# Feature tiles that overlap in the middle, and B turned straight from DRAM, in a fused S5 scan and gated unit

## The chip, the cores and the metric

One core of one Trainium2 chip runs the kernel. The metric is device time in microseconds (us) of one execution, as the median of several. The engines are TensorE (PE in the profile, its weight loads PEld), VectorE (DVE), ScalarE (ACT), GpSimd (POOL) and SyncE (SP), which issues nearly all DMAs.

## The reference

2048 tokens of 448 features are normalised; one branch runs a diagonal complex recurrence (S5) over them, the other a gated unit of width 1792; the output joins both.

```python
xn = layernorm(A_x)                                # [1, 2048, 448], bfloat16
# S5: Lam_bar = exp(dt*Lam); B_bar = ((Lam_bar-1)/Lam)[:, None] * (B_re + 1j*B_im)
Bu = einsum("bld,pd->blp", xn, B_bar)
h[t] = Lam_bar * h[t-1] + Bu[t]                    # over 2048 tokens
s = 2 * einsum("blp,dp->bld", h, C_re + 1j*C_im).real + xn * Dskip
# gated unit
z = (sigmoid(xn @ w_gate) * (xn @ w_up)) @ w_down
out = A_x + s * silu(z)
```

## The kernel before

The tokens are cut into four chunks of 512 (`NCH`, `TC`), each of four token tiles of 128. For each chunk the kernel makes: the normalised tokens `xn` (tokens on partitions), the same turned, `xnT` (features on partitions, 448 of them as `KT` = 4 tiles), 14 blocks of the gated unit (`gu_unit`, block `ft` = 128 of the 1792 columns: products `g_ps` and `u_ps`), 4 units of B times x (`bu_unit`, written -1 to -4: products `bu`), the scan and its rotations on DVE (`bu_after`), the product with `w_down` (`emit_downs`, `d_ps`) and the product with C (`emit_ys`, `y_ps`).

**The four feature tiles.** 448 is three tiles of 128 and a rest of 64. Tiles 0 to 2 are features 0 to 383. Tile 3 holds features 384 to 447 twice, on partitions 0 to 63 and again on 64 to 127, so that the gate's rest can be multiplied from the upper half of the array and the up projection's from the lower. For this the last 64 columns of `xn` are copied to columns 448 to 511 before turning: in `ln_turn` (line 272, DVE for token tiles 0 and 1 and POOL for 2 and 3 of chunk 0) and in `ln_twice` (line 277; DVE for chunk 1, ACT for chunks 2 and 3). The weights lie accordingly: `wg` and `wu` hold rows 0 to 383 as three tiles, `wt` holds the gate's last 64 rows on partitions 0 to 63 and up's on 64 to 127.

**Turning.** Chunk 0 is turned by TensorE (line 274) into PSUM and copied out by DVE (`ln_out`, line 282); chunks 1 to 3 by DMA transposes from SBUF (line 270). B is loaded into SBUF (`load_rows`, tiles `b_re`, `b_im` under the tags `raw_re` and `raw_im`), doubled on ACT (`emit_b_twice`) and turned by eight DMA transposes (`emit_b`, line 297) into `bT`. C is loaded raw under the tags `raw_c` (c_re) and `raw_re` (c_im), turned by two sets of four DMA transposes into `tc_re` and `tc_im` (line 169), and then mixed into `ct` by `emit_c`: ACT makes a temporary (`c_tmps`, line 482) and DVE adds (line 483). The first two temporaries of `emit_c` take the room of tag `raw_im`, the third and fourth that of another pool, the fifth and sixth that of `raw_c`.

**Products in halves.** Most products use 64 of the 128 rows of the array, and a product of the upper half runs beside one of the lower. A sum in PSUM (`Sum`, line 504) takes products of both halves. Where it changes halves, a word is passed: an empty instruction in POOL's queue waits for the last product of the one half, and the first product of the other waits for it.

```python
if self.half not in (None, half):
    word = pool.nop()
    tc.add_manual_dep(word.ins, self.ins.ins.name, SYNC, reason="the other half's last product")
    tc.add_manual_dep(m.ins, word.ins.name, SYNC, reason="the other half's last product")
```

**Order.** Every engine runs its instructions in the written order (`keep_order`). `duo` makes two units at a time: the first half of the one beside the second half of the other, then the reverse. Chunk 0 runs blocks 0 to 3 in the prologue and then the pairs of `emit_line`; chunks 1 to 3 run theirs with the down product of the chunk before after the second pair:

```python
emit_line(0, ((4, 5), (6, 7), (-1, 8), (-2, 9), (-3, 10), (11, 12), (-4, 13)))
```
```python
emit_line(c, ((0, -1), (1, -2), emit_downs, (2, 3), (4, -3), (5, 6), (-4, 7), (8, 9), (10, 11), *ends))
```

`at(c, ft, cost, fn)` hangs other work behind a block: second-chunk normalisation behind (0, 7), small constants of the recurrence on POOL behind blocks 6 to 13 of chunk 0, the turns of C behind (1, 0) and (1, 1), the normalisation of chunk 2 and then three `emit_c` in the down product ("down0", "down1"). PSUM has eight banks, handed out in turn; the four `d_ps` of a down product are therefore the banks of the next pair but one, (4, -3). They are emptied by eight ACT copies (lines 764 and 766).

**Loads on SP.** In order: x of chunk 0, first weight part (columns 0 to 511, four transfers, line 122 and 126), B (four transfers), second part (512 to 1023), x of chunk 1, a turn of B, part of the third weights (1024 to 1791), another turn, the rest of the third part, skip, four turns of B, x of chunk 2; then, behind (0, 7), two turns of `xn` for chunk 1, the last two turns of B, two more of `xn`, `wd`, the raw C, the swaps `bsw` of unit -4 (line 530), and the turns of C.

Of the kernel before, what the change touches and what calls it, by code (L numbers as in the profile page):

```python
# [10 lines left out]
FP32 = mybir.dt.float32  # L11
# [6 lines left out]
D = 448  # L18
F = 1792
# [8 lines left out]
CP = D // KT  # L28
NT = S_TOK // P
NPK = 2 * D  # L30
EPS = 1e-5
TWO_PI = 2.0 * math.pi
HALF_PI = 0.5 * math.pi
# [5 lines left out]
def swap_pair(ap: bass.AP) -> bass.AP:  # L39
    step_p, n_p = ap.ap[0]  # L40
    step_m, n_m = ap.ap[1]
    step_f, n_f = ap.ap[2]
    assert n_m == 2
    return bass.AP(tensor=ap.tensor, offset=ap.offset + step_m,
                   ap=[[step_p, n_p], [-step_m, n_m], [step_f, n_f]])


def bcast_mid(ap: bass.AP, n: int) -> bass.AP:
# [15 lines left out]
def kernel(  # L64
# [48 lines left out]
    skip = w.tile([P, D], BF16, name="skip")  # L113


    def load_rows(eng, t, mat, f0, f1):
        eng.dma_start(out=t[:, 0:3, f0:f1], in_=mat[0:384, f0:f1].rearrange("(kt p) f -> p kt f", p=P))
        eng.dma_start(out=t[0:64, 3, f0:f1], in_=mat[384:448, f0:f1])

    def load_w(eng, f0, f1, between=None):  # L120
        for t, mat in ((wg, B_w_gate), (wu, B_w_up)):
            eng.dma_start(out=t[:, :, f0:f1], in_=mat[0:384, f0:f1].rearrange("(kt p) f -> p kt f", p=P))
        if between:
            between()
        for mat, p0 in ((B_w_gate, 0), (B_w_up, 64)):
            eng.dma_start(out=wt[p0:p0 + 64, f0:f1], in_=mat[384:448, f0:f1])

    pool.memset(ident[:], 0.0)
    pool.affine_select(out=ident[:], in_=ident[:], compare_op=ALU.not_equal, fill=1.0, base=0,  # L129
# [17 lines left out]
            x_t.append(w.tile([P, TPC, D], BF16, name="x3", tag="tc_re"))  # L147
        sync.dma_start(out=x_t[c][:], in_=x_src[:, c * TPC:(c + 1) * TPC, :])

    for nm, mat in (("b_re", A_B_re), ("b_im", A_B_im)):  # L150
        raw[nm] = w.tile([P, KT, DP], BF16, name=nm, tag="raw" + nm[1:])
        load_rows(sync, raw[nm], mat, 0, D)
    dve.memset(raw["b_re"][:, :, D:DP], 0.0)
    load_w(sync, 512, 1024)
    load_x(1)

    ctr = {}
# [98 lines left out]

    def ln_norm(c, j):
        t = c * TPC + j
        xb = xn[c % 3]
        if c < 2:  # L260
            dve.tensor_scalar(out=xb[:, j, 0:D], in0=x_t[c][:, j, :], scalar1=mv[:, t, 0:1],
                              scalar2=rsd[:, t, :], op0=ALU.subtract, op1=ALU.mult)
        else:
            act.activation(xb[:, j, 0:D], x_t[c][:, j, :], ACT.Identity, bias=nmr[:, t, :],
                           scale=rsd[:, t, :])

    def ln_turn(c, j):
        xb, cols = xn[c % 3], slice(j * P, (j + 1) * P)
        if c > 0:
            sync.dma_start_transpose(out=xnT[c][:, 0:KT, cols], in_=xb[:, j, :])  # L270
            return
        (dve if j < 2 else pool).tensor_copy(out=xb[:, j, D:DP], in_=xb[:, j, 384:D])
        for kt in range(KT):
            pe.transpose(tps[j % 2][:, kt, :], xb[:, j, kt * P:(kt + 1) * P], ident[:])  # L274

    def ln_twice(c, copy, j0=0, j1=TPC):
        copy(out=xn[c % 3][:, j0:j1, D:DP], in_=xn[c % 3][:, j0:j1, 384:D])
        for j in range(j0, j1):
            ln_turn(c, j)

    def ln_out(j):
        dve.tensor_copy(out=xnT[0][:, :, j * P:(j + 1) * P], in_=tps[j % 2][:])  # L282

    def emit_b_twice():
        t = raw["b_im"]
        act.copy(out=t[:, 0:3, D:DP], in_=t[:, 0:3, 384:D])
        act.copy(out=t[0:64, 3, D:DP], in_=t[0:64, 3, 384:D])

    def emit_b(cc, pt):
        n = P if pt < 3 else 64
        if cc == 0:
            p0 = pt * P
        else:
            p0 = D if pt == 3 else 512 + pt * P
        sync.dma_start_transpose(out=bT[:, :, p0:p0 + n], in_=raw[("b_re", "b_im")[cc]][0:n, pt, :])

    def bu_cols(pt, cc):
        if pt == 3:  # L300
            return 384, 512
        return (pt * P, (pt + 1) * P) if cc == 0 else (512 + pt * P, 512 + (pt + 1) * P)

# [100 lines left out]

    def emit_skip(c):

        t = xn[c % 3][:, :, 0:D]
        dve.tensor_tensor(out=t, in0=t, in1=bcast_mid(skip[:], TPC), op=ALU.mult)  # L410

# [45 lines left out]
    def emit_c(i):  # L457
        pt = i // 2
        tre, tim = ctr["c_re"][:, pt, :], ctr["c_im"][:, pt, :]
        if pt == 3:  # L460
            ta, sa, tb, sb = tre, K["cr3"][:, 0:1], tim, K["nci2"][:, 3:4]
        elif i % 2 == 0:
            ta, sa, tb, sb = tre, K["cr2"][:, pt:pt + 1], tim, K["nci2"][:, pt:pt + 1]
        else:
            ta, sa, tb, sb = tim, K["ncr2"][:, pt:pt + 1], tre, K["nci2"][:, pt:pt + 1]

        if not c_room:
            for nm in ("raw_im", "raw_c"):
                both = []
                c_room.extend((nm, both, k) for k in range(2))  # L470
                if nm == "raw_im":
# [10 lines left out]
        act.activation(tmp, tb, ACT.Copy, scale=sb)  # L482
        return lambda: dve.scalar_tensor_tensor(out=ct[:, i, :], in0=ta, scalar=sa, in1=tmp, op0=ALU.mult, op1=ALU.add)
# [49 lines left out]
    def bu_unit(c, pt):  # L533
# [2 lines left out]
        sums = [Sum(t, 7) for t in psts]  # L536

        def ops(h, cc, n):
            lo, hi = bu_cols(pt, cc)
            return [(sums[cc], (bT[HALF[h], kt, lo:hi], xnT[c][HALF[h], kt, :], 0, TC))  # L540
                    for kt in range(n)]

        if pt < 3:
            u.top = ops(0, 0, 4) + ops(0, 1, 3)
# [146 lines left out]

    def gu_halves(c, ft, gt, ut, first, n0=0, n1=TC):
        f0, f1 = ft * P, (ft + 1) * P
        for t, p0 in ((gt, 0), (ut, 64)):
            pe.matmul(t[:, n0:n1], lhsT=wt[p0:p0 + 64, f0:f1],  # L695
                      rhs=xnT[c][p0:p0 + 64, 3, n0:n1], start=first, stop=not first)

    def gu_wholes(c, ft, gt, ut, first, n0=0, n1=TC, which=(0, 1)):
        f0, f1 = ft * P, (ft + 1) * P
        for t, wm in [((gt, wg), (ut, wu))[i] for i in which]:  # L700
            for kt in range(3):
                pe.matmul(t[:, n0:n1], lhsT=wm[:, kt, f0:f1], rhs=xnT[c][:, kt, n0:n1],  # L702
                          start=(first and kt == 0), stop=(not first and kt == 2))


    def gu_out(ft, gt, ub):
# [11 lines left out]
    def gu_unit(c, ft):  # L718
# [5 lines left out]

        def ops(h, i, tail):
            x = xnT[c]
            o = [(sums[i], ((wg, wu)[i][HALF[h], kt, f], x[HALF[h], kt, :], 0, TC)) for kt in range(3)]
            return o + [(sums[i], (wt[HALF[h], f], x[HALF[h], 3, :], 0, TC))] * tail

        u.top = ops(0, 0, 1) + ops(0, 1, 0)  # L730
        u.bot = ops(1, 0, 0) + ops(1, 1, 1)
# [57 lines left out]

    def y_ops(c, j, rows, d0=0, d1=D, skipped=False):  # L790
        sl = slice(j * P, (j + 1) * P)
        o = [(ident[rows, :], xn[c % 3][rows, j, d0:d1], d0, d1)] if skipped else []
# [20 lines left out]

    def emit_two(c, j):

        xb, two = xn[c % 3][:, j:TPC:2, 0:D], slice(j, TPC, 2)
        o = op_.tile([P, 2, D], BF16, name="o_t")
        for i in range(2):
            dve.tensor_tensor(out=o[:, i, :], in0=ys[c, j + 2 * i][:], in1=xb[:, i, :], op=ALU.add)  # L819
# [7 lines left out]

    def emit_rest_of(c, j):
        t = op_.tile([P, D], BF16, name="t_g", tag="zb", bufs=4)
        dve.tensor_tensor(out=t[:], in0=xn[c % 3][:, j, 0:D], in1=gs[c][:, j, :], op=ALU.mult)  # L830
        if j % 2 == 0:
            room_of_rests.append(w.tile([P, 2, D], FP32, name="t_x", tag=("raw_re", "raw_im")[j // 2]))
# [62 lines left out]
    def ln_plan(c):  # L895
# [16 lines left out]
        at(own, "down0", 0.0, lambda: ln_twice(c, act.copy))  # L912

    dummy = w.tile([P, 1], FP32, name="dummy")
    act.activation(dummy[:], hpi[:], ACT.Exp)
# [59 lines left out]
    for pt in (0, 1, 3):  # L975
        emit_sin(pt)
        emit_cos(pt)
        if pt == 0:
            emit_neg(pt)
        if pt == 0:  # L980
            emit_b_twice()
    ubs = [fp.tile([P, TC], BF16, name="ub") for _ in range(4)]

    def up_copy(ft):
# [17 lines left out]
    for t in (TPC, TPC + 2):  # L1002
# [1 line left out]
        ln_stats(t + 1)  # L1004
        ln_var(t, 2)
        emit_mul()
    emit_b(0, 0)
    load_w(sync, 1024, F, lambda: emit_b(1, 0))
    sync.dma_start(out=skip[:], in_=A_Dskip.partition_broadcast(P))
    for pt in range(1, KT - 1):  # L1010
        for cc in range(2):
            emit_b(cc, pt)
    load_x(2)


    def second_chunk(j0):
        ln_pow(TPC + j0, 2)
        for j in (j0, j0 + 1):
            ln_norm(1, j)
        ln_twice(1, dve.tensor_copy, j0, j0 + 2)  # L1020

    at(0, 7, 1.0, lambda: second_chunk(0))
    at(0, 7, 0.0, lambda: [emit_b(cc, KT - 1) for cc in range(2)])
    at(0, 7, 1.0, lambda: second_chunk(2))
    at(0, 7, 0.0, lambda: sync.dma_start(out=wd[:], in_=B_w_down.rearrange("(ft p) d -> p ft d", p=P)))
    at(0, 7, 0.0, lambda: load_c("c_re", A_C_re, A_C_im))
# [123 lines left out]
```

## Time and profile before

| what | value |
|---|---|
| time, median of 3 runs | 184.43 us (184.3 to 184.78) |
| span of the profiled execution | 182.6 us |
| median less that span (before the first and behind the last instruction) | 1.83 us |
| busy: PE / DVE / ACT / POOL | 177.7 / 165.0 / 114.1 / 24.5 us |
| prologue, before the first product in halves | 14.2 us |
| granted TensorE clock | 1.000 |
| DMA, SP's queue | 27,632 packets, 14.79 MB |

Times of single instructions count from the start of the span of the profiled execution. The runs' times also hold what lies on both sides of the span; the table's third row is that difference. A line of the timeline gives start, duration, engine, source line, operation, output and inputs, shapes and count, and in brackets the idle time of the engine before it and what ended it. "SPq" is SP issuing a DMA: its duration is the issue, not the transfer. A line of the waits gives who waited for whom, the total, the number of times and the longest.

### The profile page before, as it was taken

The page shows a single profiled execution, that of the slowest core. Times are in us where ns is not written, and L with a number is a line of the kernel's source. Part 1 is how long each engine was busy: PE and PEld are TensorE (multiplying, and loading weights), DVE is VectorE, ACT ScalarE, POOL GpSimd, SP SyncE. Part 2 cuts the span into 40 slices and gives each one's busy share as a digit, 9 for nine tenths or more (in the row PEclk, how much of TensorE's full clock was granted, in tenths as well). Part 3 has the DMA queues.
Part 4 walks back from the last instruction along what each step waited for, and adds up shares of the span by engine and source line. Part 5 has one row for each costly group of instructions (what it writes and reads, how often), then busy time and mean ns, then how long its engine had stood idle before and what let it go on. Part 6 is the DMA issues. An engine that isn't in the chain of part 4 may idle for free.

```text
span 182.6 us, 4348 instructions
## 1 busy us (share of the span) xinstructions
PE 177.7 (97%) x1644; PEld 98.3 (54%) x1644; DVE 165.0 (90%) x337; ACT 114.1 (63%) x236; POOL 24.5 (13%) x61
## 2 busy tenths in 40 slices
PE   7999999999999999999999999999999999999992
PEld 7776644446654444645654445545665544645552
DVE  4899999799989979999999999599999999699983
ACT  3999577979487787997367766057048567144100
POOL 4768546321000000004000000000000000000000
PEclk9999999999999999999999999999999999999999
DMA  5999997895434113011251010030001000011112
GB/s 152 312 307 252 231 161 106 229 311 111 104 76 89 29 32 101 4 52 52 41 79 29 4 29 0 4 101 0 4 2 29 4 13 17 4 50 50 29 36 68
DMA packets 27659, 15.07 MB, mean 83 GB/s; under 512 B 16243, under 2 KB 27638, under 8 KB 27638
## 3 DMA queue, kind: packets, MB, share of 16 engines
q1 hardware_dynamic: 27632, 14.79, 35.1%
q8 instruction: 13, 0.21, 0.5%
q14 instruction: 8, 0.07, 0.2%
q10 hardware_dynamic: 6, 0.00, 0.0%
HBM read 8.49 MB, written 1.84 MB: 57 GB/s over the span
## 4 chain that ended last, share of the span: by engine, by line
PE 97%; DVE 1%; POOL 0%; issue 0%; POOLq 0%; DVEq 0%
PE g_ps L510 25%; PE u_ps L510 19%; PE d_ps L510 17%; PE bu L510 12%; PE y_ps L510 11%; PE d_ps L1093 6%; PE warm_ps L192 2%; PE g_ps L702 2%; PE u_ps L702 1%; PE tp_x L274 1%; PE g_ps L695 1%; DVE sg L846 0%; DVE o_l L852 0%; DVE xnT L282 0%; POOL ident L129 0%
## 5 line engine op out<-in xcount | busy, mean ns | idle before, releaser
L510 PE MATMUL u_ps<-xnT,wu 64*128 64x512 bf16 x312 | 68.9, 376 | 0.0
L510 PE MATMUL g_ps<-xnT,wg 64*128 64x512 bf16 x312 | 62.0, 376 | 0.0
L740 ACT ACTIVATE sig<-g_ps 128x512 bf16<-128x512 f32 x52 | 29.1, 597 | 29.1 <-PE g_ps L510 29.1
L510 PE MATMUL bu<-xnT,bT 64*128 64x512 bf16 x196 | 45.7, 376 | 0.0
L510 PEld LDWEIGHTS <-wu 64*128 64x128 bf16 x312 | 25.3, 94 | 17.8 <-POOLq L512 1.6
L510 PE MATMUL d_ps<-wd,hF 64*128 64x448 bf16 x336 | 32.9, 349 | 0.0
L510 PEld LDWEIGHTS <-wg 64*128 64x128 bf16 x312 | 22.7, 94 | 17.6 <-POOLq L512 1.9
L740 ACT CAST ub<-u_ps 128x512 bf16<-128x512 f32 x52 | 29.3, 604 | 0.8 <-DVE hF L712 0.8
L510 PEld LDWEIGHTS <-hF 64*128 64x128 bf16 x336 | 19.9, 94 | 12.1
L510 PEld LDWEIGHTS <-bT 64*128 64x128 bf16 x196 | 17.7, 94 | 10.7
L510 PE MATMUL y_ps<-ct,h 64*128 64x448 bf16 (+2 forms) x203 | 22.7, 343 | 0.0
L589 DVE TENSOR_TENSOR_SCAN wv<-r_col,st,ta 128x512 bf16<-128x512 f32 x18 | 22.6, 1274 | 0.1
L737 DVE TENSOR_TENSOR hF<-sig,ub 128x512 bf16<-128x512 bf16 x52 | 20.9, 416 | 1.3 <-ACT ub L740 1.1
L510 PE MATMUL u_ps<-xnT,wt 64*128 64x512 bf16 x52 | 19.6, 376 | 0.0
L510 PE MATMUL g_ps<-xnT,wt 64*128 64x512 bf16 x52 | 19.6, 376 | 0.0
L510 PEld LDWEIGHTS <-h 64*128 64x128 bf16 (+1 forms) x203 | 13.4, 95 | 8.0
L570 ACT CAST bus<-bu 128x512 bf16<-128x512 f32 x24 | 14.3, 595 | 2.3 <-PE g_ps L510 2.3
L764 ACT ACTIVATE sigd<-d_ps 128x448 bf16<-128x448 f32 x12 | 6.6, 550 | 12.4 <-PE d_ps L510 12.4
L238 POOL TENSOR_TENSOR rsd<-ve,mhalf 128x1 f32<-128x1 f32 (+2 forms) x8 | 7.5, 932 | 48.5 <-PE u_ps L510 45.6
L510 PEld LDWEIGHTS <-wt 64*128 64x128 bf16 x104 | 9.8, 94 | 5.5 <-DMA wt<-in_B_w_up_dram 0.4
L1093 PE MATMUL d_ps<-wd,hF 128*128 128x448 bf16 x56 | 10.9, 353 | 0.0
L819 DVE TENSOR_TENSOR o_t<-y_ps,xn 128x448 bf16<-128x448 f32 x12 | 6.9, 618 | 3.7 <-PE y_ps L510 3.7
(153 smaller groups left out, 229.8 us busy)
## 6 DMA issues: line engine op xcount, KB each, us to landing
wd<-in_B_w_down_dram SPq DMA_DIRECT2D x1, 1568.0 KB, 7.6
x<-in_A_x_dram SPq DMA_DIRECT2D x3, 448.0 KB, 5.5
out_dram<-o_t SPq DMA_DIRECT2D x6, 224.0 KB, 2.1
wg<-in_B_w_gate_dram SPq DMA_DIRECT2D x2, 384.0 KB, 4.4
wu<-in_B_w_up_dram SPq DMA_DIRECT2D x2, 384.0 KB, 5.3
wg<-in_B_w_gate_dram SPq DMA_DIRECT2D x1, 576.0 KB
wu<-in_B_w_up_dram SPq DMA_DIRECT2D x1, 576.0 KB, 8.6
bsw<-bus SPq DMA_DIRECT2D x8, 64.0 KB, 2.0
```

The source lines that it names most:

```text
L192: pe.matmul(warm_ps[:], lhsT=ident[:], rhs=ident[:], start=True, stop=True)
L238: pool.tensor_tensor(out=rsd[:, t:t + n, :], in0=ve[:, t:t + n, :], in1=mhalf[:, 0:n, :], op=ALU.pow)
L274: pe.transpose(tps[j % 2][:, kt, :], xb[:, j, kt * P:(kt + 1) * P], ident[:])
L510: m = pe.matmul(self.t[:, n0:n1], lhsT=lhsT, rhs=rhs, start=self.done == 1, stop=self.done == self.n)
L570: empty = [lambda cc=cc: act.copy(out=bus[:, cc, :], in_=pst[cc][:]) for cc in range(2)]
L589: dve.tensor_tensor_scan(out=T["wv"][:, cc, :], data0=rb, data1=T["ta"][:, cc, :], initial=(0.0 if c == 0 else st[pt][:, cc, :]), op0=mul, ...
L702: pe.matmul(t[:, n0:n1], lhsT=wm[:, kt, f0:f1], rhs=xnT[c][:, kt, n0:n1], start=(first and kt == 0), stop=(not first and kt == 2))
L737: dve.tensor_tensor(out=h[:], in0=sig[:], in1=ub[:], op=ALU.mult)
L740: u.empty = [lambda: act.activation(sig[:], gt[:], ACT.Sigmoid), lambda: act.copy(out=ub[:], in_=ut[:])]
L764: act.activation(sigd[:], ds[j][:], ACT.Sigmoid)
L819: dve.tensor_tensor(out=o[:, i, :], in0=ys[c, j + 2 * i][:], in1=xb[:, i, :], op=ALU.add)
L1093: pe.matmul(ds[j][:], lhsT=hF[c, ft][:, j * P:(j + 1) * P], rhs=wd[:, ft, :], start=ft == 0, stop=ft == FT - 1)
```

## The change

The four feature tiles start at features 0, 128, 192 and 320 (`K_ROWS`), each 128 long, so that tiles 1 and 2 share features 192 to 255. The gate uses tiles 0, 2 and 3 whole and the upper half of tile 1 (features 128 to 191); up uses tiles 0, 1 and 3 whole and the lower half of tile 2 (features 256 to 319). Nothing is doubled by a copy any more: chunk 0's transposes read overlapping columns of `xn`; for chunks 1 to 3 the normalisation writes 512 columns (features 0 to 255, then 192 to 447) in one instruction with two overlapping runs. Skip, gate and sum read `xn` as two runs of 224. The weights' rows are rearranged to match, and one part is six transfers instead of four.

B is not loaded to SBUF: four DMA transposes read DRAM, each all 448 rows and 256 columns (tiles 0 and 1, or 2 and 3, of one of B_re and B_im). Two POOL copies behind block 9 of chunk 0 gather the last 64 columns of both into `b3` for unit -4. The second weight part is columns 512 to 1279 and stands ahead of x of chunk 1; the third, 1280 to 1791, stands behind the four turns of B. With B's raw tiles gone, `emit_c`'s first two temporaries take tag `raw_re`, and one of the last chunk's temporaries takes `raw_c`.

```diff
+HD = D // 2
+K_ROWS = (0, 128, 192, 320)
+GATE_K, UP_K = (0, 2, 3), (0, 1, 3)
+def two_runs(ap: bass.AP, step: int, n: int) -> bass.AP:
+    return bass.AP(tensor=ap.tensor, offset=ap.offset, ap=[*ap.ap[:-1], [step, 2], [1, n]])
...
+    def load_w(eng, f0, f1):
...
+        eng.dma_start(out=wg[:, 1:3, f0:f1], in_=rows(B_w_gate, 192, 448))
+        eng.dma_start(out=wg[:, 0, f0:f1], in_=rows(B_w_gate, 0, 128))
+        eng.dma_start(out=wu[:, 0:2, f0:f1], in_=rows(B_w_up, 0, 256))
+        eng.dma_start(out=wu[:, 2, f0:f1], in_=rows(B_w_up, 320, 448))
+        eng.dma_start(out=wt[0:64, f0:f1], in_=rows(B_w_gate, 128, 192))
+        eng.dma_start(out=wt[64:128, f0:f1], in_=rows(B_w_up, 256, 320))
...
-    for nm, mat in (("b_re", A_B_re), ("b_im", A_B_im)):
-        raw[nm] = w.tile([P, KT, DP], BF16, name=nm, tag="raw" + nm[1:])
-        load_rows(sync, raw[nm], mat, 0, D)
-    dve.memset(raw["b_re"][:, :, D:DP], 0.0)
-    load_w(sync, 512, 1024)
+    load_w(sync, 512, 1280)
...
+            xb, src = two_runs(xb, 2 * P, 2 * P), two_runs(src, 192, 2 * P)
...
-        (dve if j < 2 else pool).tensor_copy(out=xb[:, j, D:DP], in_=xb[:, j, 384:D])
         for kt in range(KT):
-            pe.transpose(tps[j % 2][:, kt, :], xb[:, j, kt * P:(kt + 1) * P], ident[:])
+            pe.transpose(tps[j % 2][:, kt, :], xb[:, j, K_ROWS[kt]:K_ROWS[kt] + P], ident[:])
-    def ln_twice(c, copy, j0=0, j1=TPC):
-        copy(out=xn[c % 3][:, j0:j1, D:DP], in_=xn[c % 3][:, j0:j1, 384:D])
...
+    def emit_b(cc, kt):
+        sync.dma_start_transpose(out=bT[:, kt:kt + 2, cc * D:(cc + 1) * D],
+                                 in_=(A_B_re, A_B_im)[cc][:, K_ROWS[kt]:K_ROWS[kt] + 2 * P])
+    b3 = w.tile([P, KT, P], BF16, name="b3")
+    def emit_b3():
+        for cc in range(2):
+            pool.tensor_copy(out=b3[:, :, cc * 64:(cc + 1) * 64], in_=bT[:, :, cc * D + 384:(cc + 1) * D])
...
-            for nm in ("raw_im", "raw_c"):
+            for nm in ("raw_re", "raw_c"):
...
-        if pt == 0:
-            emit_b_twice()
...
-    emit_b(0, 0)
-    load_w(sync, 1024, F, lambda: emit_b(1, 0))
+    for cc in range(2):
+        for kt in (0, 2):
+            emit_b(cc, kt)
+    load_w(sync, 1280, F)
     sync.dma_start(out=skip[:], in_=A_Dskip.partition_broadcast(P))
-    for pt in range(1, KT - 1):
-        for cc in range(2):
-            emit_b(cc, pt)
     load_x(2)
...
     at(0, 7, 1.0, lambda: second_chunk(0))
-    at(0, 7, 0.0, lambda: [emit_b(cc, KT - 1) for cc in range(2)])
+    at(0, 9, 0.0, emit_b3)
     at(0, 7, 1.0, lambda: second_chunk(2))
```

More of the change, by code (lines that the diff above doesn't have):

```diff
@@ L113, with rows @@
     skip = w.tile([P, D], BF16, name="skip")
[L116 to L126, printed above, removed]
+    def load_w(eng, f0, f1):
+        def rows(mat, r0, r1):
+            m = mat[r0:r1, f0:f1]
+            return m.rearrange("(kt p) f -> p kt f", p=P) if r1 - r0 > P else m
+        eng.dma_start(out=wg[:, 1:3, f0:f1], in_=rows(B_w_gate, 192, 448))
[4 more added lines that the diff above has]
+        eng.dma_start(out=wt[64:128, f0:f1], in_=rows(B_w_up, 256, 320))
     pool.memset(ident[:], 0.0)
@@ L258, in ln_norm, with xn_runs @@
         t = c * TPC + j
-        xb = xn[c % 3]
+        xb, src = xn[c % 3][:, j, :], x_t[c][:, j, :]
+        if c == 0:
+            xb = xb[:, 0:D]
+        else:
+            xb, src = two_runs(xb, 2 * P, 2 * P), two_runs(src, 192, 2 * P)
         if c < 2:
-            dve.tensor_scalar(out=xb[:, j, 0:D], in0=x_t[c][:, j, :], scalar1=mv[:, t, 0:1],
-                              scalar2=rsd[:, t, :], op0=ALU.subtract, op1=ALU.mult)
-        else:
-            act.activation(xb[:, j, 0:D], x_t[c][:, j, :], ACT.Identity, bias=nmr[:, t, :],
-                           scale=rsd[:, t, :])
+            dve.tensor_scalar(out=xb, in0=src, scalar1=mv[:, t, 0:1], scalar2=rsd[:, t, :], op0=ALU.subtract,
+                              op1=ALU.mult)
+        else:
+            act.activation(xb, src, ACT.Identity, bias=nmr[:, t, :], scale=rsd[:, t, :])
+    def xn_runs(c, j):
+        return two_runs(xn[c % 3][:, j, :], HD if c == 0 else DP - HD, HD)
     def ln_turn(c, j):
@@ L271, in ln_turn, with b_cols @@
             return
-        (dve if j < 2 else pool).tensor_copy(out=xb[:, j, D:DP], in_=xb[:, j, 384:D])
         for kt in range(KT):
-            pe.transpose(tps[j % 2][:, kt, :], xb[:, j, kt * P:(kt + 1) * P], ident[:])
-    def ln_twice(c, copy, j0=0, j1=TPC):
-        copy(out=xn[c % 3][:, j0:j1, D:DP], in_=xn[c % 3][:, j0:j1, 384:D])
-        for j in range(j0, j1):
-            ln_turn(c, j)
+            pe.transpose(tps[j % 2][:, kt, :], xb[:, j, K_ROWS[kt]:K_ROWS[kt] + P], ident[:])
     def ln_out(j):
         dve.tensor_copy(out=xnT[0][:, :, j * P:(j + 1) * P], in_=tps[j % 2][:])
[L286 to L302, printed above, removed]
+    def emit_b(cc, kt):
[5 more added lines that the diff above has]
+            pool.tensor_copy(out=b3[:, :, cc * 64:(cc + 1) * 64], in_=bT[:, :, cc * D + 384:(cc + 1) * D])
+    def b_cols(rows, kt, pt, cc):
+        return b3[rows, kt, :] if pt == 3 else bT[rows, kt, cc * D + pt * P:cc * D + (pt + 1) * P]
     K = {}
@@ L407, in emit_skip @@
     def emit_skip(c):
-        t = xn[c % 3][:, :, 0:D]
-        dve.tensor_tensor(out=t, in0=t, in1=bcast_mid(skip[:], TPC), op=ALU.mult)
+        t = xn_runs(c, slice(0, TPC))
+        by = two_runs(skip[:], HD, HD).unsqueeze(1).to_broadcast((P, TPC, 2, HD))
+        dve.tensor_tensor(out=t, in0=t, in1=by, op=ALU.mult)
     dve.memset(cosT[:, :, HC - 1:HC], 1.0)
@@ L467, in emit_c @@
         if not c_room:
-            for nm in ("raw_im", "raw_c"):
+            for nm in ("raw_re", "raw_c"):
                 both = []
                 c_room.extend((nm, both, k) for k in range(2))
-                if nm == "raw_im":
+                if nm == "raw_re":
                     c_room.extend((None, None, None) for _ in range(2))
@@ L538, in ops @@
         def ops(h, cc, n):
-            lo, hi = bu_cols(pt, cc)
-            return [(sums[cc], (bT[HALF[h], kt, lo:hi], xnT[c][HALF[h], kt, :], 0, TC))
-                    for kt in range(n)]
+            return [(sums[cc], (b_cols(HALF[h], kt, pt, cc), xnT[c][HALF[h], kt, :], 0, TC))
+                    for kt in (range(KT) if n == KT else (UP_K, GATE_K)[h])]
         if pt < 3:
@@ L693, in gu_halves @@
         f0, f1 = ft * P, (ft + 1) * P
-        for t, p0 in ((gt, 0), (ut, 64)):
+        for t, p0, kt in ((gt, 0, 1), (ut, 64, 2)):
             pe.matmul(t[:, n0:n1], lhsT=wt[p0:p0 + 64, f0:f1],
-                      rhs=xnT[c][p0:p0 + 64, 3, n0:n1], start=first, stop=not first)
+                      rhs=xnT[c][p0:p0 + 64, kt, n0:n1], start=first, stop=not first)
     def gu_wholes(c, ft, gt, ut, first, n0=0, n1=TC, which=(0, 1)):
         f0, f1 = ft * P, (ft + 1) * P
[L700 to L703, printed above, removed]
+        for t, wm, kts in [((gt, wg, GATE_K), (ut, wu, UP_K))[i] for i in which]:
+            for k, kt in enumerate(kts):
+                pe.matmul(t[:, n0:n1], lhsT=wm[:, k, f0:f1], rhs=xnT[c][:, kt, n0:n1],
+                          start=(first and k == 0), stop=(not first and k == 2))
     def gu_out(ft, gt, ub):
@@ L726, in ops @@
             x = xnT[c]
-            o = [(sums[i], ((wg, wu)[i][HALF[h], kt, f], x[HALF[h], kt, :], 0, TC)) for kt in range(3)]
-            return o + [(sums[i], (wt[HALF[h], f], x[HALF[h], 3, :], 0, TC))] * tail
+            o = [(sums[i], ((wg, wu)[i][HALF[h], k, f], x[HALF[h], kt, :], 0, TC))
+                 for k, kt in enumerate((GATE_K, UP_K)[i])]
+            return o + [(sums[i], (wt[HALF[h], f], x[HALF[h], 1 + i, :], 0, TC))] * tail
         u.top = ops(0, 0, 1) + ops(0, 1, 0)
@@ L791, in y_ops @@
         sl = slice(j * P, (j + 1) * P)
-        o = [(ident[rows, :], xn[c % 3][rows, j, d0:d1], d0, d1)] if skipped else []
+        o = [(ident[rows, :], xn_runs(c, j)[rows, d // HD, :], d, d + HD) for d in range(d0, d1, HD)] if skipped else []
         for pt in range(3):
@@ L814, in emit_two @@
     def emit_two(c, j):
-        xb, two = xn[c % 3][:, j:TPC:2, 0:D], slice(j, TPC, 2)
+        two = slice(j, TPC, 2)
         o = op_.tile([P, 2, D], BF16, name="o_t")
         for i in range(2):
-            dve.tensor_tensor(out=o[:, i, :], in0=ys[c, j + 2 * i][:], in1=xb[:, i, :], op=ALU.add)
+            dve.tensor_tensor(out=two_runs(o[:, i, :], HD, HD), in0=two_runs(ys[c, j + 2 * i][:], HD, HD),
+                              in1=xn_runs(c, j + 2 * i), op=ALU.add)
         dve.tensor_tensor(out=o[:], in0=o[:], in1=gs[c][:, two, :], op=ALU.mult)
@@ L829, in emit_rest_of @@
         t = op_.tile([P, D], BF16, name="t_g", tag="zb", bufs=4)
-        dve.tensor_tensor(out=t[:], in0=xn[c % 3][:, j, 0:D], in1=gs[c][:, j, :], op=ALU.mult)
+        dve.tensor_tensor(out=two_runs(t[:], HD, HD), in0=xn_runs(c, j), in1=two_runs(gs[c][:, j, :], HD, HD),
+                          op=ALU.mult)
         if j % 2 == 0:
-            room_of_rests.append(w.tile([P, 2, D], FP32, name="t_x", tag=("raw_re", "raw_im")[j // 2]))
+            room_of_rests.append(w.tile([P, 2, D], FP32, name="t_x", tag=("raw_re", "raw_c")[j // 2]))
         rests[j] = room_of_rests[j // 2][:, j % 2, :]
@@ L911, in ln_plan @@
             at(own, "down0", 0.0, lambda j=j: ln_norm(c, j))
-        at(own, "down0", 0.0, lambda: ln_twice(c, act.copy))
+        at(own, "down0", 0.0, lambda: [ln_turn(c, j) for j in range(TPC)])
     dummy = w.tile([P, 1], FP32, name="dummy")
@@ L1019, in second_chunk @@
             ln_norm(1, j)
-        ln_twice(1, dve.tensor_copy, j0, j0 + 2)
+        for j in (j0, j0 + 1):
+            ln_turn(1, j)
     at(0, 7, 1.0, lambda: second_chunk(0))
-    at(0, 7, 0.0, lambda: [emit_b(cc, KT - 1) for cc in range(2)])
+    at(0, 9, 0.0, emit_b3)
     at(0, 7, 1.0, lambda: second_chunk(2))
```

## The prediction

> **What bounds the kernel now.** I read the page's busy times and its chain first, then TensorE's waits after the prologue.
>
> ```profile
> PE 177.7 (97%) x1644; PEld 98.3 (54%) x1644; DVE 165.0 (90%) x337; ACT 114.1 (63%) x236; POOL 24.5 (13%) x61
> PE 97%; DVE 1%; POOL 0%; issue 0%; POOLq 0%; DVEq 0%
> ```
>
> TensorE (PE) is busy 97% of the span and is 97% of the chain, at a granted clock of 1.000. After 14.2 us its 64-row products start in pairs every 0.2155 us. The change alters neither their number nor their shape, so time comes only from the prologue (0 to 14.2), from stalls of PE, or from new ones. The waits of the weight loads from 14 to 60 us:
>
> ```profile
> PEld L510 <- POOLq L512: 1.1, 3, 0.4
> PEld L510 <- DMA wt<-in_B_w_up_dram: 0.4, 1, 0.4
> ```
>
> One wait on data (21.4 to 21.85 us, `wt` of block 8), and waits on the Pool words of line 512: a word stands in Pool's queue, so whatever is queued there ahead of it can hold PE.
>
> **1. The doubled tail columns go (prologue).** The timeline around 9 us:
>
> ```profile
> 8.71 0.40 DVE L261 TENSOR_SCALAR xn<-x,mv,rsd 128x448 bf16<-128x448 bf16 x1 [0.44 <-POOL rsd L238]
> 9.16 0.24 POOL L272 COPY xn<-xn 128x64 bf16<-128x64 bf16 x1 [0.30 <-DVE xn L261]
> 9.22 0.93 DVE L282 COPY xnT<-tp_x 128x512 bf16<-128x512 bf16 x2
> ```
>
> Token tile 3's fourth transpose waits for the Pool copy's end, 9.40, and ends at 9.69. Three transposes start 0.06 apart from 9.16; the fourth would follow at 9.34 and, taking 0.23, end at 9.57: 0.12 earlier. The copies of tiles 0 and 1 on DVE (0.19 and 0.21) mostly lie in waits: the first in that for `rsd` and `tp_v`, the second before a transpose's end at 6.27, which it moves by 0.06. So DVE, which is a chain without gaps from line 282 to the sign of sine 2 (15.25 to 15.59), comes 0.18 earlier; the mirror copy that needs that sign is the last thing before the first Pool words (15.63), and PE's second half of pair (4,5) starts with them at 15.70. PE alone would gain 0.26, but the words cap it. Term: -0.18 (bounds -0.05 and -0.26).
>
> **2. Second weight part to 1280.** `wt` of block 8 now lies in the part that before lands by 13.6. From 15.70 to 26.40 PE does 49 pairs: 49 x 0.2155 = 10.56 of 10.70; the loss is 0.14, and the two streams lose 0.10 and 0.21 at 21.85. Term: -0.16 (bounds -0.10 and -0.32). Weights are six transfers instead of four, three times: 6 more issues at 0.6 = 3.6 us of SP. They replace four B loads (2.3) and eight turns (12.2); up to x of chunk 1 the count stays 16.
>
> **3. B turned from DRAM.** No turn from DRAM is in this trace. Turns from SBUF hold SP 1.19 to 2.24 us, median 1.28, 64-row ones (1.79, 1.19) no less than 128-row ones. Four at 1.28, or by bytes (448 x 256 against 128 x 512 elements, 1.75 times) 2.24, or by source rows (3.5 times) 4.5 each. From 9.75 the last is issued at 13.6, 16.5 or 23.2 and lands 2.4 to 5.4 later. PE reads B's imaginary half at 20.9. I take the first, nearest to the 64-row turns: zero, covered by 20.9 - 19.0 = 1.9 us. The third weight part's issues then run from 14.9 to 18.5. The longest landing of a weight transfer is 8.6: main rows by 23.5 to 25.3, tails by 27.1, against reads of block 10 at 26.4 and 27.7. Zero too, and up to +1 where the turns hold SP by bytes.
>
> **4. A new wait on ScalarE.** `emit_c` put its first two temporaries into tag `raw_im`, free since B was turned. Now they take `raw_re`, where raw C_im lies until all four turns of `tc_im` have read it. Queued behind them in ACT: a third temporary and the eight copies that empty the four `d_ps` banks. PE needs those banks for pair (4,-3): the fourth one at 55.26. ACT and SP before:
>
> ```profile
> 45.23 0.40 ACT L277 COPY xn<-xn 128x256 bf16<-128x256 bf16 x1
> 48.22 1.23 ACT L482 ACTIVATE c_tmps<-tc_re,nci 128x448 f32<-128x448 bf16 x2 [2.58 <-DMA tc_re<-c_re]
> 49.35 0.65 ACT L482 ACTIVATE c_tmp<-tc_re,nci 128x448 f32<-128x448 bf16 x1
> ...
> 53.30 0.55 ACT L766 CAST zb<-d_ps 128x448 bf16<-128x448 f32 x1
> ```
> ```profile
> 37.49 1.11 SPq L530 DMA_DIRECT2D bsw<-bus  x1
> 38.65 0.60 SPq L531 DMA_DIRECT2D bsw<-bus  x1
> 41.16 5.78 SPq L169 DMA_TRANSPOSE tc_re<-c_re  x4
> 47.04 5.86 SPq L169 DMA_TRANSPOSE tc_im<-c_im  x4
> ```
>
> From the temporaries' start to the last bank emptied: 53.85 - 48.22 less 0.29 of idle = 5.3. So any start after 55.26 - 5.3 = 49.96 stalls PE one for one. When does `tc_im` land? SP loses the two B turns at 25.90 to 28.98 and 0.7 more, so wd and C load 3.7 us earlier: c_re lands near 37.4 instead of 41.09. `bus` of unit -4 is ready at 36.38; two swap issues (1.1 at best) give 37.65 as start of `tc_re` (before: 41.16). From there to the release by `tc_im` it was 54.19 - 41.16 = 13.0; with the quickest four turns of the trace (5.14, xnT at 52.99) and a landing 2.5 after the last issue, 11.5. Landing: 49.2 to 50.7; stall 0 to 0.74. Both sets of C turns took 5.8, the long end, so I take +0.50. DVE's gates wait along, but DVE stood idle 0.84 there for `tc_im`.
>
> **5. B3 on Pool.** Two 128x256 copies (`cosT`, 128x255: 0.40 each) go ahead of `emit_a` in Pool's queue, beside block 9. Before:
>
> ```profile
> 25.44 0.20 POOL L380 TENSOR_TENSOR a_re<-r_col,cs 128x4 f32<-128x4 f32 x1 [1.58 <-PE u_ps L510]
> 25.73 0.55 POOL L381 TENSOR_SCALAR a_re<-a_re 128x4 f32<-128x4 f32 x1
> 26.25 0.72 POOL L382 TENSOR_TENSOR a_im<-r_col,sn 128x4 f32<-128x4 f32 x1
> ```
>
> The next words pass at 27.46, when PE's own products release them. A word passes once the operation ahead is handed over, as L382 was when L381 began (25.73). With 0.80 added that is 26.5: 0.9 us of cover, zero. The same size of operation takes 0.20 or 0.72, so the copies may stretch; upper end +0.9.
>
> **6. No cost.** Chunk 1's norms grow by 1/7 (0.35 each, +0.2 for four) and lose two copies of 0.19. Chunks 2 and 3: four norms on ACT, 2.73, grow by at most 0.39 and lose a copy of 0.40, all ahead of step 4's wait. Two-run skip, gate and sum keep their elements; if the 1.06 us skip doubled, DVE's 3.7 us of waits for `y_ps` would cover it. The skip product of the last tile stays one per half.
>
> **Sum.** 182.6 - 0.18 - 0.16 + 0.50 = 182.76 of span. The median of the runs, 184.43, lies 1.83 above this span; with that, 184.6. A measurement of this kernel tells about 0.3%, 0.55 us, from no change.
>
> **The rivals.**
> *The wait stays hidden* (C's turns land before 49.96, at 11.5 after 37.65): 184.43 - 0.34 = 184.1, and 183.85 at the terms' outer bounds, faster than the 0.3%. For it: the xnT set of 5.14. Against it: both C sets. 0.28, of which 0.16 beyond 0.3%.
> *The ACT wait is longer*, the other side: if wd and C don't come earlier, `tc_re` starts at 41.16 and temporaries at 54.2: stall 4.2, 188.3; halfway, 186.2. It is slower by 0.3% once `tc_im` lands after 50.9. For it: the temporaries already waited 2.58 for `tc_re` before. 0.18.
> *Pool's words come late*: +0.5 to +0.9 on the forecast, 185.1 to 185.5, decided where the copies end Pool's queue after 27.5. For it: 0.55 and 0.72 beside DVE's bf16 products against 0.20. The Trainium skill (SBUF — State Buffer, Who interferes with whom) says that a DVE instruction with two SBUF inputs fully blocks a GpSimd one that reads SBUF, for the whole instruction; those rows look like it, and by the rule each copy could wait for one DVE product. 0.14.
> *B lands late*: at 4.5 us per turn the last lands at 25.6 to 28.6, 5 to 8 us late: 189 to 192; by bytes B and the third weight part are at most 1.0 late each, 185.6 to 186.6. Against it: the 64-row turns. The Trainium skill (DMA: Bandwidth & Descriptors, Why small descriptors are slow) holds that 256-byte pieces from HBM pay about a quarter more, which pieces between SBUFs do not; no run here shows it. 0.10.
>
> **How the numbers follow.** Forecast 0.30, 184.6, its own range 184.1 to 185.0, all within 0.3%. Faster 0.16; same 0.30 + 0.12 = 0.42; slower 0.18 + 0.14 + 0.10 = 0.42. The range leaves out late B (0.10) and the upper half of the longer wait (0.09): 183.8 to 186.6.
>
> **What would show it.** Right: no wait on `wt` near 21 us; ACT's temporaries waiting for C_im's turns until about 50; a gap of PE near 55, the size of the change in span plus 0.34. Wrong: a PE gap near 20.5 (B), near 27.5 with the word late (Pool), or none near 55.

## The result and the profile after

The changed kernel takes 186.78 us (median of four runs, 185.98 to 188.06) where the kernel before, measured beside it, took 184.37: a ratio of 1.0139 (95% interval 1.0094 to 1.0184; the two medians give 1.0131), 1.4% slower, 0.18 us above the upper end of the range. Its profiled execution took 187.28 us with a span of 185.4, 2.8 longer than the span before; it is 0.5 slower than the median, so the spans differ by a little more than the medians' 2.4. The page's span, PE's busy time and the shares of the chain:

```profile
span 185.4 us, 4343 instructions
PE 178.1 (96%) x1644; PEld 102.4 (55%) x1644; DVE 164.8 (89%) x332; ACT 113.0 (61%) x232; POOL 27.6 (15%) x61
PE 70%; DVE 11%; SPq 7%; DMA 7%; ACT 3%; issue 1%; POOL 0%; DVEq 0%; POOLq 0%; ACTq 0%
```

PE had 97% of the chain before. Now 14% of it are DMA issues (SPq) and transfers (DMA), and 14% DVE and ACT: the chain that ended last runs back from PE through ACT into the turns of C. Two waits make it so; from 14 to 30 us, and from 40 to 62 us:

```profile
PEld L509 <- POOLq L511: 2.1, 2, 1.5
PE g_ps L509 <- POOLq L511: 1.1, 2, 1.0
```
```profile
ACT c_tmps L481 <- DMA tc_im<-c_im: 6.8, 1, 6.8
PE u_ps L509 <- ACT zb L765: 0.5, 1, 0.5
```

No line names `wt` any more. How the difference builds up is read from the starts of PE's first products into a tile, before against after: first `bu` 20.25 and 20.10 (-0.15); first `d_ps` 41.00 and 41.87 (+0.87); first `y_ps` 72.24 and 74.89 (+2.65); last product 179.02 and 181.67 (+2.65). So two stretches cost time: 1.02 net between 20 and 41 us, and 1.78 between 41 and 72. From 72 us to PE's last product nothing differs.

**The first stretch.** One step of PE's pairs, at 25.87, lasts 1.45 instead of 0.2155 (mean of the two streams): 1.24 lost, less some 0.2 that the wait for `wt` had cost.

```profile
25.87 0.39 PE L509 MATMUL g_ps<-xnT,wg 64*128 64x512 bf16 x1 [0.97 <-POOLq L511]
```

Pool and DVE around it, after:

```profile
23.27 2.49 POOL L366 TENSOR_SCALAR t<-den 128x4 f32<-128x4 f32 x1
26.37 0.94 POOL L297 COPY b<-bT 128x256 bf16<-128x256 bf16 x2
```
```profile
22.07 1.38 DVE L268 TENSOR_SCALAR xn<-x,mv,rsd 128x512 bf16<-128x512 bf16 x4
23.36 1.09 DVE L736 TENSOR_TENSOR hF<-sig,ub 128x512 bf16<-128x512 bf16 x3
24.37 0.68 DVE L574 TENSOR_TENSOR ta<-bus,cosT 128x1024 bf16<-128x1024 bf16 x1
24.97 0.68 DVE L578 TENSOR_TENSOR tb<-bus,spm 128x1024 bf16<-128x1024 bf16 x1
25.68 0.69 DVE L581 TENSOR_TENSOR ta<-ta,tb 128x1024 bf16<-128x1024 bf16 x1
```

The same two places before:

```profile
23.34 0.24 POOL L368 TENSOR_SCALAR t<-den 128x4 f32<-128x4 f32 x1
```
```profile
23.78 0.20 DVE L277 COPY xn<-xn 128x128 bf16<-128x128 bf16 x1
23.89 1.09 DVE L737 TENSOR_TENSOR hF<-sig,ub 128x512 bf16<-128x512 bf16 x3
```

An operation on four columns takes 2.49 us instead of 0.24. It is the fourth of `emit_den` (behind block 8, untouched by the change), and the words that PE waits for stand behind it. It lasts as long as DVE's five products with two inputs in SBUF, which follow each other without a pause from 23.36 to 25.65. Before, those began at 23.89, when the operation was over (23.58). The change made DVE 0.5 earlier there, 0.4 of it by taking the copies of line 277 out of DVE's chain (22.21 to 23.89 before, 22.07 to 23.36 after), while Pool stayed where it was. That the earlier products caught the operation is read from the two traces; no run gave DVE the 0.4 back.

**The second stretch.** ACT and SP, after:

```profile
43.34 2.95 ACT L271 ACTIVATE xn<-x,nmr,rsd 128x512 bf16<-128x512 bf16 x4
53.05 1.23 ACT L481 ACTIVATE c_tmps<-tc_re,nci 128x448 f32<-128x448 bf16 x2 [6.76 <-DMA tc_im<-c_im]
...
57.71 0.58 ACT L765 CAST zb<-d_ps 128x448 bf16<-128x448 f32 x1
```
```profile
38.89 5.93 SPq L172 DMA_TRANSPOSE tc_re<-c_re  x4
44.92 5.12 SPq L172 DMA_TRANSPOSE tc_im<-c_im  x4
```

The temporaries wait 6.76 us for C_im's turns. ACT empties the four banks at 55.68, 56.55, 57.42 and 58.29, and PE's pair (4,-3) makes its first product into each of them 0.05 later, the last two at 57.47 and 58.34. These two after, and the same products before:

```profile
57.47 0.37 PE L509 MATMUL bu<-xnT,bT 64*128 64x512 bf16 x1
58.34 0.37 PE L509 MATMUL u_ps<-xnT,wu 64*128 64x512 bf16 x1 [0.49 <-ACT zb L765]
```
```profile
55.26 0.38 PE L510 MATMUL bu<-xnT,bT 64*128 64x512 bf16 x1
55.69 0.38 PE L510 MATMUL u_ps<-xnT,wu 64*128 64x512 bf16 x1
```

So the bank that is emptied last is that of `u_ps`, which PE wanted at 55.69 before and, 0.87 late, at 56.56 now: 58.34 - 56.56 = 1.78, the whole second stretch. The prediction took 55.26, which is when the third bank is wanted.

### The profile page after: what moved, and what is told of

Its sections match the earlier page's. It is cut to its first block, busy times and chain, and to the rows that moved or that the text cites. A ratio compares the mean times of both kernels' runs of the same rounds, so it can differ in the third digit from the quotient of the medians.

```text
span 185.4 us, 4343 instructions
## 1 busy us (share of the span) xinstructions
PE 178.1 (96%) x1644; PEld 102.4 (55%) x1644; DVE 164.8 (89%) x332; ACT 113.0 (61%) x232; POOL 27.6 (15%) x61
## 4 chain that ended last, share of the span: by engine, by line
PE 70%; DVE 11%; SPq 7%; DMA 7%; ACT 3%; issue 1%; POOL 0%; DVEq 0%; POOLq 0%; ACTq 0%
PE g_ps L509 18%; PE u_ps L509 14%; PE d_ps L509 11%; PE y_ps L509 11%; PE bu L509 7%; PE d_ps L1092 6%; SPq L172 5%; DMA c_re<-in_A_C_im_dram 4%; DMA tc_im<-c_im 2%; PE warm_ps L195 2%; DVE hF L710 2%; DVE ub L984 1%; DVE stats L211 1%; SPq L279 1%; ACT zb L765 1%
## 5 line engine op out<-in xcount | busy, mean ns | idle before, releaser
L509 PE MATMUL bu<-xnT,bT 64*128 64x512 bf16 x168 | 38.5, 376 | 0.5 <-ACT zb L765 0.5
L509 PEld LDWEIGHTS <-bT 64*128 64x128 bf16 x168 | 15.4, 94 | 8.6 <-issue 0.9
```

The lines of the kernel that those rows point to most:

```text
L509: m = pe.matmul(self.t[:, n0:n1], lhsT=lhsT, rhs=rhs, start=self.done == 1, stop=self.done == self.n)
```

## The experiments

Ratios are to the kernel before, run on the same chip in the same job. "The changed kernel" has line 467 `for nm in ("raw_re", "raw_c")` and `(8, 0.0, emit_den)`.

**Only the room of ACT's temporaries** (`e1_room`):

```diff
-            for nm in ("raw_re", "raw_c"):
+            for nm in ("raw_c", "raw_re"):
...
-                if nm == "raw_re":
+                if nm == "raw_c":
```

> The changed kernel, but emit_c's first two temporaries take raw_c (raw C_re, free once tc_re is turned, which they read anyway) and the next two raw_re. Theory: the wait of 6.8 us on tc_im in ACT goes, PE's gaps at 55.7 to 58.3 us (1.9 in sum) go, Pool's late word at 24.7 to 25.9 stays: 186.8 - 1.9 = 184.9 (184.5 to 185.3). Rival (the DMA queue is late, whatever room is taken): the gap at 56 stays and the time stays near 186.8.

Measured 185.90, ratio 1.0072 (1.0053 to 1.0090). ACT, as far as it replaces the line with the wait above:

```profile
46.65 1.23 ACT L481 ACTIVATE c_tmps<-tc_re,nci 128x448 f32<-128x448 bf16 x2
```

No wait, and no gap of PE near 56. So the wait is the room's alone. Against the changed kernel it wins 0.9 by the medians, 1.2 by the ratios and 1.3 by the profiled spans, and not the 1.78 of the stall or the 1.9 expected: Pool's gap stays (1.45 at 25.87), and a second late word at 29.36 costs 0.45 here.

**Only the place of the denominators** (`e2_den`), ahead of the stretch of products:

```diff
-    for ft, cost, fn in (..., (8, 0.0, emit_den), ...
+    for ft, cost, fn in (..., (6, 0.0, emit_den), ...
```

> The changed kernel, but emit_den's five Pool operations hang behind block 6 of chunk 0 instead of block 8. Theory: the gap of PE at 25.9 (1.24 us) goes, since no Pool operation stands before the words while DVE runs its products of two SBUF inputs at 23.4 to 26.3. But the turns of C start when raw c_re has landed (38.8), which does not move, so PE reaches the banks 1.1 us earlier and waits that much longer there: 186.8 - 1.24 + 1.1 = 186.6 (186.0 to 187.0). Rival (the word is held by the b3 copies or by B, not by the 128x4 operation): gap at 25.9 unchanged. A second rival, gaps simply add: 185.5.

Measured 186.73, ratio 1.0125 (1.0103 to 1.0147): nothing won, as the theory said, although the gap at 25.87 is gone and PE starts `d_ps` at 40.49, 1.38 earlier. The wait grew:

```profile
ACT c_tmps L481 <- DMA tc_im<-c_im: 7.6, 1, 7.6
```

The last turn of C_im landed at 52.42 (52.97 in the changed kernel), since the landing of C, not PE, sets when it comes. PE arrives earlier and stalls longer: from `d_ps` to `y_ps` it takes 2.6 more than before the change, instead of 1.78 more.

**Both** (`e3_both`):

> Both edits of the two runs before. Theory: both gaps go: 186.8 - 1.24 - 1.9 = 183.7 (183.4 to 184.2), that is 0.3% below the kernel before, by the prologue (-0.15) and the wait on wt (-0.16). Rival (B from DRAM or the two-run patterns cost something of their own): above 184.4.

Measured 184.51, ratio 1.0003 (0.9991 to 1.0016). The whole slowdown is in these two places: 2.5 by the ratios (2.27 by the medians), where the one alone wins 1.2 (0.9) and the other nothing that can be told (0.3, and 0.05). The changed kernel's own ratio is known only to 0.0045, or 0.8 us. The forecast of 183.7 was too low: the gain in prologue and weights, 0.3, doesn't show. In its profile PE starts the second half of blocks 4 and 5 at 15.87, 0.16 later than before, behind a late word (some 0.2 lost).

**The room alone in the kernel before** (`e4_before_room`), to see ACT's wait without the rest:

```diff
-            for nm in ("raw_im", "raw_c"):
+            for nm in ("raw_re", "raw_c"):
```

> The kernel before with one edit: emit_c's first two temporaries take raw_re instead of raw_im, so they wait for C_im's turns. Theory: tc_im lands at 54.1 as before, temporaries start then, and the last of the four banks is empty 5.3 later, at 59.4, where PE wants it at 55.3: +4.1, so 188.5 (187.5 to 188.9). Rival (ACT's wait is absorbed, since ACT is busy 63% only): under 185.5.

Measured 189.69, ratio 1.0274 (1.0250 to 1.0298). The temporaries waited 8.8 us, until 54.24, which by the prediction's threshold of 49.96 stalls PE for 4.28. With the last bank wanted at 55.69 the threshold is 50.39, less the 0.18 by which PE came earlier here, and the stall 4.03. Between `d_ps` and `y_ps` PE took 36.95 us instead of 31.24: 5.7 more. The windows after the stall have the rest (columns: window and its length, busy time and count of PE, PEld, DVE, ACT and POOL, granted clock, DMA share, GB/s):

```profile
54.00:59.50 5.50, 2.37 (x15) 0.78 (x12) 2.12 (x5) 5.26 (x12) 0.00 (x0) 1.00 0.47 95
59.50:63.00 3.50, 3.47 (x18) 1.45 (x19) 3.43 (x8) 2.62 (x6) 0.00 (x0) 0.51 0.00 0
```

Behind the stall TensorE is granted half its clock for some 3.4 us; pairs come every 0.43, and 1.7 us go once more. So the stall itself is 4.0, one for one; this one cost 1.7 more than its length.

**The second weight part alone** (`e5_before_w`):

```diff
-    load_w(sync, 512, 1024)
+    load_w(sync, 512, 1280)
...
-    load_w(sync, 1024, F, lambda: emit_b(1, 0))
+    load_w(sync, 1280, F, lambda: emit_b(1, 0))
```

> The kernel before with one part of the change alone: the second weight part reaches to row 1280 instead of 1024, the third begins there. By the theory of the prediction the wait for the 64-row weights near 21.4 us goes and nothing else moves: 0.16 us less, ratio 0.999, 184.0 to 184.4 where the kernel before takes 184.4. The rival: the larger second part is late for the first pair that reads it, or pushes B's loads and turns back, and a new gap of PE stands between 20 and 23 us: over 184.7.

Measured 184.39 against 184.23, ratio 1.0013 (0.9988 to 1.0039): inconclusive for 0.16, since the interval is wider. Its profiled execution took 187.3, and nothing is read from its trace.

**Is it the place on Pool, or what is done there?** (`e6_read`, `e7_write`, `e10_fills`; both repairs, and behind block 8 something that nobody reads). In `e6_read` it is `emit_den`'s five operations on tiles of its own, in `e7_write` five fills over four tiles, in `e10_fills` six fills of one tile:

```diff
+    def emit_den_again():
+        t = col("den_b")
+        for _ in range(6):
+            pool.memset(t[:], 0.0)
...
-    for ft, cost, fn in ((6, 0.0, emit_constants), (6, 0.0, emit_den), ...
+    for ft, cost, fn in ((6, 0.0, emit_constants), (6, 0.0, emit_den), (8, 0.0, emit_den_again), ...
```

> The kernel with both repairs (184.5) and, at block 8, where the changed kernel has the denominators, five more Pool operations of the same 128x4 shapes on tiles that nobody reads; the real denominators stay at block 6. Theory: the place on Pool alone makes the stall, since one of the five comes up while VectorE runs products with two SBUF inputs back to back: one takes over 2 us instead of 0.2, the words behind it are late, PE has a gap of 1.2 us near 25.9, and the time is 185.7 (185.3 to 186.1). The rival: the gap in the changed kernel came from the denominators' results being late for their readers, or from the copy of B's columns; then five unread operations cost nothing, 184.5 (184.2 to 184.8).

Measured 186.19, ratio 1.0109 (1.0095 to 1.0124), and the fourth of the unread operations is shut out just as in the changed kernel:

```profile
23.41 2.47 POOL L376 TENSOR_SCALAR t_b<-den_b 128x4 f32<-128x4 f32 x1
```

PE loses 1.15 at 26.0, and 0.5 more at 29.55, where the Pool operations pushed back hold the next words; that second loss is why it is 1.7 and not the 1.2 expected. The results' readers have no part in it.

> As the run before, but the five extra Pool operations at block 8 are fills of 128x4 with a constant, which read no SBUF. If only Pool operations that read SBUF are shut out by VectorE's products, each fill takes about 0.2 us, PE has no gap near 25.9, and the time is 184.5 (184.2 to 184.9). The rival: any Pool operation that touches SBUF is shut out, one fill takes over 1 us, and the time is 185.7 (185.3 to 186.1).

Measured 184.47, ratio 1.0013 (0.9996 to 1.0030). As expected, but it tells less than meant: the five fills were over by 23.05, before DVE's products began. Hence the next:

> As the run with five fills, whose fills were all over by 23.05 us, ahead of VectorE's run of products with two SBUF inputs (23.4 to 25.8). Here six fills of 128x4 go one after the other on one tile, each after the last (0.28 apart in that run), so that from about 22.5 they reach to 24.2, into the products. If a fill, which reads no SBUF, isn't shut out, they end by 24.3, the words behind them pass in time, and it is 184.5 (184.2 to 184.9). The rival: any Pool operation that touches SBUF is shut out; the fill that comes up after 23.4 ends near 25.8, PE has a gap of over 1 us there, and it is 186.0 (185.6 to 186.4).

Measured 184.54, ratio 1.0013 (0.9999 to 1.0026). Pool's fifth fill, and DVE beside it:

```profile
23.31 0.10 POOL L373 MEMSET den_b<- 128x4 f32 x1
```
```profile
23.12 1.09 DVE L741 TENSOR_TENSOR hF<-sig,ub 128x512 bf16<-128x512 bf16 x3
```

It runs in the midst of the products and takes 0.10, as does the sixth at 23.47. A Pool operation that only writes isn't held by these products; the one that reads SBUF was, until DVE's first pause (0.03 us, behind 25.65 in the changed kernel and 25.80 in `e6_read`).

How long a reader is held differs, though. Later in the changed kernel each of Pool's readers got in after about one DVE operation, although these followed each other without a pause:

```profile
27.56 1.12 POOL L379 TENSOR_SCALAR a_re<-a_re 128x4 f32<-128x4 f32 x1
28.65 1.06 POOL L380 TENSOR_TENSOR a_im<-r_col,sn 128x4 f32<-128x4 f32 x1
```
```profile
27.50 1.09 DVE L409 TENSOR_TENSOR xn<-xn,skip 128x1792 bf16<-128x1792 bf16 x1 [0.70 <-DMA skip<-in_A_Dskip_dram]
28.50 2.33 DVE L587 TENSOR_TENSOR_SCAN wv<-r_col,ta 128x512 bf16<-128x512 f32 x2
```

And in the kernel before, line 380 took 0.20 at 25.44, where `ta` (24.90 to 25.58) and `tb` (25.50 to 26.18) of the same five products meet. What decides between one operation and a whole run stays open.

**The late first words** (`e8_mirror`; both repairs, and):

```diff
-    for pt in (0, 1, 3, 2):
+    for pt in (0, 1, 3):
         emit_mirror(pt)
...
+    at(0, 5, 0.0, lambda: emit_mirror(2))
```

> The kernel with both repairs and one more move: Pool's mirror copies of the fourth table, which wait for VectorE's sign of sine 2 and stand ahead of the first words, go behind block 5. Theory: the words are then there when the second half of blocks 4 and 5 asks for them, PE's gap of 0.4 us near 15.9 goes, and the time is 184.2 (183.9 to 184.5), just under the kernel before. The rival: the start is held by something else as late (the evictions of the first blocks, or a later word behind the moved copies), and nothing moves: 184.5 or more.

Measured 185.08, ratio 1.0060 (1.0047 to 1.0073): slower. Both sides were right in part. The gap near 15.9 is gone, but the moved copies push the denominators back into another product of DVE (line 710, tanh and `ub`, 18.32 to 19.01), and the words of blocks 6 and 7 behind them come 1.1 late at 19.21:

```profile
18.35 0.75 POOL L366 TENSOR_SCALAR t<-den 128x4 f32<-128x4 f32 x1
```

**The denominators in the prologue** (`e9_best`; as the last, and):

```diff
     emit_steps()
+    emit_den()
...
-    for ft, cost, fn in ((6, 0.0, emit_constants), (6, 0.0, emit_den), ...
+    for ft, cost, fn in ((6, 0.0, emit_constants), ...
```

> Both repairs, the mirror copies of the fourth table behind block 5 as in the run before, and the denominators moved from block 6 into the start, behind the step angles, where Pool has nothing to do from 10.9 to 12.8 us. Theory: with the denominators ahead of no word, the words of blocks 6 and 7 (over 1 us late in the run before) are in time, the 0.4 us won near 15.9 stay, PE has no gap over 0.1 us between 14 and 33 us: 184.0 (183.7 to 184.3), below the kernel before. The rival: the moved mirror copies alone make those words late, or the denominators push the first mirror copies and the words near 15 us: 184.6 or more.

Measured 184.11, ratio 0.9980 (0.9967 to 0.9994), span 182.0. Pool's wait of 1.9 us there takes all five operations, and PE has no gap over 0.1 us from 14 to 33 us. `bu` starts at 19.85, `d_ps` at 40.29, `y_ps` at 71.53, 0.4 to 0.7 ahead of the kernel before: 0.2% faster than it, with the change in. Whether the same moves on Pool would speed up the kernel before as well was not tried, so the 0.2% is not the worth of the change; the nearest measure of that is `e3_both`, 1.0003.

## Why the prediction was wrong, point by point

**The sum** had +0.16 on the span; it was +2.8. Two of its terms failed, the +0.50 for the wait on ScalarE and the nothing for Pool's words; each gave a gap of over a microsecond.

**Step 4, the wait on ScalarE: right mechanism, mis-sized term.** Forecast +0.50, that is a start of the temporaries at 50.46; they started at 53.05, and PE lost 1.78. What failed was the landing, in two parts. C's raw tiles landed at 38.82 instead of 37.4 (`wd` was issued at 28.91, 2.75 earlier than before and not 3.7), so the turns of `tc_re` began at 38.89, not 37.65: 1.24. Then 14.16 us passed to the release, where the forecast allows 12.81 and its long end 13.0: 1.35. The turns took 5.93 and 5.12, and the last one landed 4.2 after its issue instead of 2.5; that 1.7 alone is about the size of the stall. Two errors went the other way: the last bank was wanted 0.43 later than the prediction read (55.69, not 55.26), and PE came 0.87 late. Together, 0.50 + 1.24 + 1.35 - 0.43 - 0.87 = 1.79. The slope, one for one, held: with a threshold of 50.39, moved by as much as PE was early or late, the stalls come out at 1.79, 2.61 and 4.03 in the changed kernel, `e2_den` and `e4_before_room`, where 1.78, 2.61 and 4.0 were measured.

**Step 5, and the rival of Pool's late words: wrong place.** The copies of B took 0.60 and 0.40 beside block 9, and PE has no gap behind them: the cover of 0.9 held. Step 1 and step 6 moved DVE earlier by removing copies, and the sum counted that as DVE's own business. It didn't ask which Pool operations the earlier products would now lie beside. The answer was in the rows of before: line 368 ended at 23.58 and the products began at 23.89, 0.3 us apart. The rival named the right mechanism and priced it 0.5 to 0.9 at 27.5; it struck at 25.87 for 1.24, and not through the copies that step 5 weighed but through an operation that the change had not touched.

By the Trainium skill (SBUF — State Buffer, Who interferes with whom) a DVE instruction with two SBUF inputs contends with a GpSimd one that reads SBUF and not with one that only writes. Both halves agree with the runs: 2.47 us for the reading operation in `e6_read`, 0.10 for the fill in `e10_fills`. The prediction read it as a wait for one DVE product per operation; here it was a run of five, 2.3 us, though of other readers about one (1.12 and 1.06 above).

**Step 1, the prologue: not shown.** In the changed kernel's profiled execution the second half of pair (4,5) came at 15.56 instead of 15.71: -0.15 against -0.18. But one pair of traces can't show a term of this size. Six experiments have the same prologue, and there it came at 15.32 (`e2_den`, `e10_fills`), 15.56, 15.70, 15.77 and 15.87; in `e4_before_room`, with the old prologue, at 15.70. Why equal prologues differ by half a microsecond stays open. PE's clock is not the whole of it: the five warm-up products near 6.1 took 0.74 in `e3_both` (15.87), which is slow, but 0.44 in `e7_write` (15.77), as in the changed kernel.

**Step 2, the second weight part: shown in the profile, not in time.** No wait names `wt`; a gain of 0.16 can't be told in `e5_before_w`.

**Step 3, B from DRAM: right.** SP's timeline of after:

```profile
9.36 4.87 SPq L290 DMA_TRANSPOSE bT<-in_A_B_re_dram  x2
14.27 3.25 SPq L290 DMA_TRANSPOSE bT<-in_A_B_im_dram  x2
```

The four held SP 1.38, 3.45, 1.91 and 1.29, 8.0 together: nearer the 2.24 that bytes give than the 1.28 taken. The last landed at 20.14, ahead of the read at 20.9, with 0.8 of cover left instead of 1.9, and PE has no gap there. The third weight part's issues ended at 20.82 instead of 18.5, and nothing waited for it. Skip landed late by 0.7 for DVE, off the path.

**Step 6: right on ACT.** The four norms on ACT took 2.95 (2.73 and a copy of 0.40 before). What chunk 1's norms on DVE did is under step 5.

**The rivals.** The longer ACT wait and Pool's late words both came true, at a price below the lower end of the one (a stall of 1.78 against 2.1 to 4.2) and above the upper end of the other. That the range of the first, 186.2 to 188.3, holds the measured 186.78 is luck: ACT's stall by itself makes 185.9, and the rest is Pool's. Each had been priced as if it came alone, 0.18 and 0.14. They aren't additive: as `e2_den` shows, time lost ahead of a wait for a transfer is mostly absorbed by it, and time won there is given back.

## What to carry to other kernels

When a change takes work off one engine's chain, list what its neighbours do at the new times, not only what they wait for: here a freed 0.5 us on DVE laid its products over a Pool operation that PE's next word stood behind. A tag is a wait: before giving a temporary another tile's room, write down when that tile's last reader lands, with the slow end of each duration, and what stands in the engine's queue behind it. And repair two stalls in a row together before judging either, since the later one hides what the earlier repair wins.

## What the runs showed of the hardware that was not expected

- A Pool operation on 128x4 elements that reads SBUF lasted 2.47 to 2.49 us when it came up as a run of five back-to-back DVE products with two SBUF inputs began; it was not let in between two of them. Others were, after about one DVE operation (1.12 and 1.06 us). Fills ran beside the products in 0.10.
- After a stall of PE of about 4 us the granted clock was halved for one stretch of some 3.4 us (0.51 in the window from 59.5 to 63.0 of `e4_before_room`); in the profiled executions of the changed kernel and of `e2_den`, whose stalls were 1.8 and 2.6, there is no such stretch.
- The last turn of C_im landed 4.2 us after its issue in the changed kernel, 4.4 in `e2_den` and 4.0 to 4.5 in `e3_both`, `e7_write`, `e8_mirror` and `e10_fills`, where 2.4 to 2.5 is usual. In all six the records have a transfer of instructions of 0.9 to 1.6 us that begins 1.2 to 2.1 after the issue (at 50.85 and 49.37 in the first two). In `e1_room` and `e6_read` that transfer came at 51.26 and 51.99, when the last turn had landed or nearly so (51.33 and 51.38), and the turn took 2.4. That the one delays the other was not tried and stays open.
- A turn from DRAM of 448 rows by 256 columns held SP for 1.29 to 3.45 us: four equal ones, and none like the next. The second was the longest in every profiled execution of the changed kernel and its variants (3.0 to 3.7).
